# Whole loads of a batch's first x tile, four taps in superblock 4, and transposes moved apart in superblocks 8 to 11

## The chip, the cores and the metric

The kernel runs on one core of a Trainium2 chip. The core has TensorE (matmuls; its weight loads are listed as PEld), VectorE (DVE), ScalarE (ACT), GpSimd (POOL) and SyncE (SP, which here only issues DMAs), and 16 DMA engines that all queues share. The metric is the device time of one execution in microseconds. Of the kernel before, 8 executions were timed: median 751.04 us, from 749.45 to 758.43.

## The reference

Two steps on 32768 tokens (8 batches of 4096) of 192 features. The first is a causal convolution with 7 taps, whose weights differ for each token and each of 8 heads and are a softmax over the taps. The second is a feed-forward layer of width 2048 with `h - tanh(h)` between its two matrix products.

```python
# x: (8, 4096, 192); weight_gen: (8, 4096, 8 heads, 7 taps); group = 24 features of a head
w = softmax(weight_gen, axis=-1)
x_pad = concatenate([zeros((B, 6, D)), x], axis=1)     # a batch begins with six zero rows
x_unf = x_pad[:, arange(S)[:, None] + arange(7)[None, :], :]
y = einsum('bshk,bskhg->bshg', w, x_unf.reshape(B, S, K, H, group))
h = y.reshape(32768, 192) @ w_in                       # 192 x 2048
out = (h - tanh(h)) @ w_out                            # 2048 x 192
```

## The kernel before

**Tiling.** The tokens are cut into 32 superblocks of 1024, four to a batch, numbered n = 0 to 31. Partition p of a tile holds 8 consecutive tokens. A superblock's x tile has 6 more rows in front (the halo), so partition p also has the six tokens before its own; in a batch's first superblock (n = 0, 4, 8, ...) partition 0 has zeros there.

**The convolution of one superblock.** ScalarE takes the exponentials of the weights (line 154), VectorE sums them, takes the reciprocals and scales (lines 168, 183, 214). GpSimd multiplies x by the weights, tap by tap, into bf16 products (line 255): taps 0 to 3 into `pa`, taps 4 to 6 into `pb`. From n = 4 on (`HELP`) VectorE does the eighth token of taps 0 and 1 (line 289). Then the products are added over the taps in two ways together. Some additions are accumulating DMAs issued on GpSimd's queue (`dma_sum`, line 221). The rest is done by TensorE: it transposes each remaining tap's products by multiplying with an identity and accumulates them in PSUM (line 338, 24 matmuls a tap). How many taps are left for TensorE depends on n:

- n in `PART` (2, 3, 4): one sum inside `pa`, taps 0 and 1 plus taps 2 and 3 (768 KB), issued before `pb`'s product. TensorE transposes taps 4, 5, 6, 0, 1.
- n = 5 to 12: one sum of `pb` into `pa[0:3]` (1152 KB), issued after `pb`'s product. TensorE transposes taps 3, 0, 1, 2.
- n in `TWO_SUMS` (13 to 31): that sum and, a superblock later (`second_sum`), `pa[2:4]` into `pa[0:2]`. TensorE transposes two.

The result is evicted from PSUM into `convT` (line 364) in two pieces: `t2`, chunks 0 and 1 of the 192 features, and `t1`, chunk 2.

**The feed-forward layer.** The main loop of superblock n runs over 16 f tiles of 128 hidden features. For each, `gemm1` writes `ph` with 6 matmuls (line 381), ScalarE takes the tanh (394), VectorE subtracts into `gt` (395). The second product runs a superblock behind as a stream of pairs of matmuls into two PSUM banks `obank` (line 417), evicted by ScalarE (436) and stored by SP (440), one store a superblock. `ph` and the transposes' `pc` share three PSUM slots in turn.

**What sets the order.** The schedule is by hand: each engine runs its instructions in program order. A plan says how many output pairs follow each f tile (`pairs`), at which f tile and after how many pairs each transpose piece of superblock n + 1 is put (`t1`, `t2`), and where VectorE's softmax sums and scale stand. `FIRST` is for n = 1, `STEADY` for all others:

```python
STEADY = dict(pairs=(5, 11, 0, 16, 4, 12, 6, 10, 0, 6, 10, 8, 8, 8, 8, 16), t1=(14, 8), t2=(13, 0), scale=14, sums=(1, 13))
```

GpSimd runs ahead: during superblock n it makes the products of n + 2. On SP's queue stand, in program order, the loads of x (n + 3) and of later weights, and the store of n - 1. Up to n = 8 the loads come after the store in the program, from n = 9 on before it. An x load waits for its slot (two x tiles) and, by a manual dependency (`x_after`), for GpSimd's first product of the superblock before.

**A batch's first x tile** is loaded by four DMAs: partitions 16 to 127 whole, partitions 0 to 15 without halo, the halo of partitions 1 to 15, and zeros for the halo of partition 0 (lines 121 and 131, called at 143 to 149).

## Time and profile before

| | |
|---|---|
| median of 8 executions | 751.04 us |
| the profiled execution | 750.1 us |
| its span in the trace | 748.3 us |
| mean granted TensorE clock | 0.998 |
| HBM read, written | 54.49 MB, 25.17 MB |

The span is the time between the first and last instruction recorded; the rest of the execution lies around it. A slice is a fortieth of the span. A digit is the busy share in tenths, where 9 is 90% or more; PEclk is the clock granted to TensorE, in tenths of its full speed.

```profile
PE   3899999999999989999999999999999999999997
...
DVE  7999899989999969999999999999999999988893
ACT  4888888888888868898989989898898989888882
POOL 7999999999999999999999999999999999992000
PEclk9999999999999999999999999999999999999999
DMA  8926636865667669887779878787988877776112
```

The costliest groups have line, engine, operation, written and read tiles, shapes and count; then busy time and mean duration of one; then idle time just before and what ended it:

```profile
L395 DVE TENSOR_TENSOR gt<-ph,th 128x1024 bf16<-128x1024 f32 x512 | 602.3, 1219 | 40.5 <-ACT th L394 27.3
L394 ACT ACTIVATE th<-ph 128x1024 f32<-128x1024 f32 x512 | 514.3, 1026 | 70.3 <-PE ph L381 59.5
L381 PE MATMUL ph<-convT,w_in 64*128 64x512 bf16 x3072 | 419.5, 379 | 4.9 <-DVE gt L395 3.4
...
L417 PE MATMUL obank<-w_out,gt 64*128 64x192 bf16 x7936 | 410.6, 243 | 4.9 <-issue 4.6
L255 POOL TENSOR_TENSOR pa<-x_t,wsm 128x3072 bf16<-128x3072 f32 (+2 forms) x63 | 341.7, 5657 | 0.2
```

Two matmuls run at a time on the two halves of TensorE's rows, so the durations of lines 381 and 417 overlap and their sum is more than TensorE's busy time.

The DMAs by what they move, with the count, the size of one and the median time from issue to landing:

```profile
x_t<-in_x_dram SPq DMA_DIRECT2D x24, 1344.0 KB, 8.1
pa<-pb POOLq DMA_DIRECT2D x27, 1152.0 KB, 9.5
out_dram<-out_sb SPq DMA_DIRECT2D x31, 768.0 KB, 4.3
pa<-pa POOLq DMA_DIRECT2D x22, 768.0 KB, 7.4
x_t<-in_x_dram SPq DMA_DIRECT2D x7, 1176.0 KB, 9.5
```

### The profile page before, as it was taken

The page shows a single profiled execution, that of the slowest core. Times are in us where ns is not written, and L with a number is a line of the kernel's source. Part 1 is how long each engine was busy: PE and PEld are TensorE (multiplying, and loading weights), DVE is VectorE, ACT ScalarE, POOL GpSimd, SP SyncE. Part 2 cuts the span into 40 slices and gives each one's busy share as a digit, 9 for nine tenths or more (in the row PEclk, how much of TensorE's full clock was granted, in tenths as well). Part 3 has the DMA queues.
Part 4 walks back from the last instruction along what each step waited for, and adds up shares of the span by engine and source line. Part 5 has one row for each costly group of instructions (what it writes and reads, how often), then busy time and mean ns, then how long its engine had stood idle before and what let it go on. Part 6 is the DMA issues. An engine that isn't in the chain of part 4 may idle for free.

```text
span 748.3 us, 30081 instructions
## 1 busy us (share of the span) xinstructions
PE 724.0 (97%) x13640; PEld 559.7 (75%) x13640; DVE 684.6 (91%) x711; ACT 640.2 (86%) x872; POOL 657.8 (88%) x158
## 2 busy tenths in 40 slices
PE   3899999999999989999999999999999999999997
PEld 2477777777777777777777777787777777877777
DVE  7999899989999969999999999999999999988893
ACT  4888888888888868898989989898898989888882
POOL 7999999999999999999999999999999999992000
PEclk9999999999999999999999999999999999999999
DMA  8926636865667669887779878787988877776112
GB/s 237 241 46 159 173 116 178 193 170 136 166 167 176 178 173 216 186 217 172 194 207 221 210 199 204 170 201 205 228 193 189 212 179 191 193 148 110 45 44 86
DMA packets 34464, 129.64 MB, mean 173 GB/s; under 512 B 4808, under 2 KB 9656, under 8 KB 30480
## 3 DMA queue, kind: packets, MB, share of 16 engines
q0 software_dynamic: 19296, 50.73, 39.5%
q1 hardware_dynamic: 15040, 77.00, 29.6%
q8 instruction: 106, 1.74, 1.0%
q14 instruction: 22, 0.18, 0.1%
HBM read 54.49 MB, written 25.17 MB: 106 GB/s over the span
## 4 chain that ended last, share of the span: by engine, by line
PE 94%; DVE 3%; issue 1%; ACT 1%; DMA 0%
PE obank L417 44%; PE ph L381 44%; PE pc L338 4%; PE po L460 1%; DVE gt L395 1%; DVE pa L255 1%; ACT th L394 1%; DVE pb L255 0%; DMA wg_t<-in_weight_gen_dram 0%; DVE obank L196 0%; DVE zsum L168 0%; PE obank L338 0%; DVE wsm L214 0%; DVE obank L214 0%; ACT wg_t L154 0%
## 5 line engine op out<-in xcount | busy, mean ns | idle before, releaser
L395 DVE TENSOR_TENSOR gt<-ph,th 128x1024 bf16<-128x1024 f32 x512 | 602.3, 1219 | 40.5 <-ACT th L394 27.3
L394 ACT ACTIVATE th<-ph 128x1024 f32<-128x1024 f32 x512 | 514.3, 1026 | 70.3 <-PE ph L381 59.5
L381 PE MATMUL ph<-convT,w_in 64*128 64x512 bf16 x3072 | 419.5, 379 | 4.9 <-DVE gt L395 3.4
L417 PEld LDWEIGHTS <-gt 64*128 64x128 bf16 x7936 | 357.5, 94 | 87.4 <-issue 13.0
L417 PE MATMUL obank<-w_out,gt 64*128 64x192 bf16 x7936 | 410.6, 243 | 4.9 <-issue 4.6
L255 POOL TENSOR_TENSOR pa<-x_t,wsm 128x3072 bf16<-128x3072 f32 (+2 forms) x63 | 341.7, 5657 | 0.2
L255 POOL TENSOR_TENSOR pb<-x_t,wsm 128x4608 bf16<-128x4608 f32 (+2 forms) x33 | 284.1, 8611 | 0.9 <-ACT wsm L206 0.5
L381 PEld LDWEIGHTS <-w_in 64*128 64x128 bf16 x3072 | 163.6, 94 | 80.3 <-issue 18.4
L436 ACT ACTIVATE out_sb<-obank 128x192 f32<-128x192 f32 x248 | 81.2, 327 | 14.7 <-PE obank L417 14.3
L364 ACT ACTIVATE convT<-pc 128x1024 bf16<-128x1024 f32 (+1 forms) x62 | 50.1, 810 | 1.2 <-PE pc L338 0.7
L221 POOL DMA_DIRECT2D pa<-pb x27 | 34.7, 1284 | 14.5 <-DVE pa L289 7.7
L338 PEld LDWEIGHTS <-pa 64*128 64x128 bf16 x2016 | 41.4, 101 | 6.9 <-DVE pa L255 1.1
L221 POOL DMA_DIRECT2D pa<-pa x22 | 35.8, 1629 | 9.3 <-DMA pa<-pb 8.4
L338 PE MATMUL pc<-ident,pa 64*128 64x64 bf16 x1920 | 40.7, 192 | 1.3 <-DVE pa L255 0.8
L168 DVE TENSOR_REDUCE zsum<-wg_t 128x32 f32<-128x224 f32 (+1 forms) x61 | 23.7, 388 | 2.8 <-ACT wg_t L154 2.8
L154 ACT ACTIVATE wg_t<-wg_t 128x448 f32<-128x448 f32 x32 | 18.3, 571 | 7.1 <-DMA wg_t<-in_weight_gen_dram 7.1
L214 DVE TENSOR_TENSOR wsm<-wg_t,pc 128x448 f32<-128x448 f32 x27 | 16.8, 621 | 3.0 <-DVE pc L183 0.5
L289 DVE TENSOR_TENSOR pa<-x_t,ph 128x384 bf16<-128x384 f32 x28 | 15.5, 554 | 1.2
L183 DVE RECIPROCAL pc<-zsum 128x64 f32<-128x64 f32 x27 | 14.9, 551 | 1.2 <-ACT convT L364 1.2
L338 PE MATMUL pc<-ident,pb 64*128 64x64 bf16 x288 | 6.3, 202 | 8.9 <-POOL pb L255 8.9
L338 PEld LDWEIGHTS <-pb 64*128 64x128 bf16 x360 | 7.8, 105 | 9.6 <-POOL pb L255 8.9
L460 PE MATMUL po<-w_out,gt 64*128 64x192 bf16 x256 | 11.2, 243 | 0.0
(27 smaller groups left out, 55.7 us busy)
## 6 DMA issues: line engine op xcount, KB each, us to landing
x_t<-in_x_dram SPq DMA_DIRECT2D x24, 1344.0 KB, 8.1
pa<-pb POOLq DMA_DIRECT2D x27, 1152.0 KB, 9.5
out_dram<-out_sb SPq DMA_DIRECT2D x31, 768.0 KB, 4.3
pa<-pa POOLq DMA_DIRECT2D x22, 768.0 KB, 7.4
x_t<-in_x_dram SPq DMA_DIRECT2D x7, 1176.0 KB, 9.5
wg_t<-in_weight_gen_dram SPq DMA_DIRECT2D x32, 224.0 KB, 7.2
x_t<-in_x_dram SPq DMA_DIRECT2D x1, 768.0 KB
w_out<-in_moe_w_out_dram POOLq DMA_DIRECT2D x1, 768.0 KB, 9.3
```

Source lines behind the costliest of these rows:

```text
L154: last_exp[0] = nc.scalar.activation(out=wg_t[:].rearrange("p j h k -> p (j h k)"), in_=wg_t[:].rearrange("p j h k -> p (j h k)"), func=AC ...
L168: nc.vector.reduce_sum(out=zsum_of[n][:, j0 * H : j1 * H], in_=e_of[n][:, j0:j1].rearrange("p j h k -> p (j h) k"), axis=AX.X,)
L221: return nc.gpsimd.dma_start(out=out.rearrange("p k j d -> p k (j d)"), in_=in_.rearrange("p k j d -> p k (j d)"), accum_op=mybir.AluOpTyp ...
L255: return eng.tensor_mul(prod(k0, k1)[:, :, j0:j1].rearrange("p k j (h g) -> p k (j h) g", h=H), bass.AP(tensor=x_v.tensor, offset=x_v.offs ...
L338: nc.tensor.matmul(pc[r][:, col : col + R] if home else pc[:, r, col : col + R], lhsT=prods[c][gi][r * R : (r + 1) * R, 2 * j : 2 * j + 2] ...
L364: last_conv[0] = nc.scalar.activation(out=out, in_=pc[:, :, 0:cols].rearrange("p r (cj t) -> p r cj t", t=R), func=ACT.Copy,)
L381: nc.tensor.matmul(ph[:, r, :], lhsT=w_in[r * R : (r + 1) * R, c, f * P : (f + 1) * P], rhs=convT[r * R : (r + 1) * R, c, :], start=(c == ...
L394: last_act[0] = nc.scalar.activation(out=th[:], in_=ph_f, func=ACT.Tanh)
L395: last_sub[0] = nc.vector.tensor_sub(gt[:], ph_f, th[:])
L417: mm = nc.tensor.matmul(po[:, 0:D], lhsT=g_of[n][f][r * R : (r + 1) * R, col : col + P], rhs=w_out[r * R : (r + 1) * R, f, :], start=(r == ...
L436: last_act[0] = nc.scalar.activation(out=out_sb[:, j, :], in_=po[:, 0:D], func=ACT.Copy)
L460: nc.tensor.matmul(po[:, r, 0:D], lhsT=g_of[n][f][r * R : (r + 1) * R, col : col + P], rhs=w_out[r * R : (r + 1) * R, f, :], start=(f == 0 ...
```

## The change

Three edits.

1. *A batch's first x tile* (n = 4, 8, ..., 28) comes in one DMA of 128 partitions with their halo. Partition 0 then holds the last rows of the batch before in its halo. The zeros are written over them by a separate DMA, which the program issues in superblock n - 3 at the first f tile from 8 on after the load. It waits for the load to land.
2. *Superblock 4* leaves `PART`: it has the sum of three taps like superblocks 5 to 12, and TensorE transposes taps 3, 0, 1, 2. It alone is in `LAST_TAP`: GpSimd makes tap 2 before and tap 3 after the sum is issued, instead of both before.
3. *Superblocks 8 to 11* follow a plan `APART`: the pieces `t2` and `t1` of superblocks 9 to 12 stand at f = 10 and f = 15 instead of 13 and 14, the output pairs are spread otherwise (128 in all, as before), and the softmax sums and the scale stand at other f tiles.

```diff
-    PART = (2, 3, 4)
+    PART = (2, 3)
+    LAST_TAP = (4,)
+    X_LATE = ()
+    ZERO_AT = 8
+    RELIEF = ()
...
         else:
-            dma = rows(16 if s == 0 else 0, P)
+            dma = rows(16 if s == 0 and ZERO_AT is None else 0, P)
             if behind is not None:
                 order(dma, behind, "order of the loads")
-            if s == 0:
+            if s == 0 and ZERO_AT is None:
                 rows(0, 16, HALO)
                 rows(1, 16, 0, HALO)
                 no_halo()
+            elif s == 0:
+                halo_of[n] = no_halo
...
-        x_after[n + 1] = mul(nc.gpsimd, 0, KH, 0, J - 1 if n in HELP else J)
-        mul(nc.gpsimd, KH, KA)
-        second_sum(n - 1)
+        first = mul(nc.gpsimd, 0, KH, 0, J - 1 if n in HELP else J)
+        if n in LAST_TAP:
+            x_after[n + 1] = mul(nc.gpsimd, KH, KA - 1)
+            second_sum(n - 1)
+        else:
+            mul(nc.gpsimd, KH, KA)
+            second_sum(n - 1)
+        if n not in LAST_TAP or n not in X_LATE:
+            x_after[n + 1] = first
...
                 dma_sum(pa[:, 0:3], pb[:, 0:3])
+                if n in LAST_TAP:
+                    mul(nc.gpsimd, KA - 1, KA)
...
+    APART = dict(pairs=(4, 12, 0, 16, 0, 16, 4, 12, 0, 16, 4, 12, 0, 6, 10, 16), t1=(15, 5), t2=(10, 2), scale=15, sums=(7, 10))
+    APART_IN = (8, 9, 10, 11)
...
-        plan = FIRST if n == 1 else STEADY
+        plan = FIRST if n == 1 else APART if n in APART_IN else STEADY
...
+            if n + 3 in halo_of and f >= ZERO_AT:
+                halo_of.pop(n + 3)()
             out_pairs(plan["pairs"][f] - done)
```

The diff also adds a function `gemm1_relieved` for f tiles in `RELIEF`; that tuple is empty, so nothing calls it. `X_LATE` is empty as well, so `x_after` keeps its meaning.

In each engine's order of instructions this comes to: TensorE has 24 transposes with their weight loads fewer. GpSimd has one product more, and in superblock 4 its sum stands after `pb`'s product. SP has 14 loads fewer. The zeros of superblock 4 stand directly behind its load; those of 8 behind the load and a load of weights; those of 12, 16, ..., 28 also behind the store that follows. VectorE and ScalarE have the same instructions in another order within superblocks 8 to 11.

## The prediction

> **What bounds the kernel now.** I read the busy shares, the chain that ended last, the chain in order of time, the waits, then single stretches by timeline and by windows. First the page:

> ```profile
> PE 724.0 (97%) x13640; PEld 559.7 (75%) x13640; DVE 684.6 (91%) x711; ACT 640.2 (86%) x872; POOL 657.8 (88%) x158
> ...
> q8 instruction: 106, 1.74, 1.0%
> ...
> PE 94%; DVE 3%; issue 1%; ACT 1%; DMA 0%
> ```

> TensorE is the bound: 94% of the chain. An edit gains only if it removes TensorE work or a stop of TensorE. The chain in order of time shows such stops. One place of each superblock (the two adjacent first-product tiles, f = 8 and 9) comes again and again:

> ```profile
> 140.83 1.43 PE ph L381 x12
> ...
> 165.04 1.43 PE ph L381 x12
> ...
> 187.53 1.38 PE ph L381 x12
> ...
> 232.42 1.38 PE ph L381 x12
> ...
> 254.86 1.38 PE ph L381 x12
> ...
> 282.06 1.34 PE ph L381 x12
> ```

> Superblocks 2 to 4 take about 23 us; then the steps are 24.21 (n = 5 to 6), 22.49, 22.44 on average to 254.86, and 27.20 (n = 10 to 11). From 12 on, where two taps instead of four are transposed, they are about 21.86. So two places lose time: 24.21 - 22.44 = 1.77 us and 27.20 - 22.44 = 4.76 us. The timeline shows the second:

> ```profile
> 264.32 0.34 SPq L121 DMA_DIRECT2D x_t<-in_x_dram  x1
> ...
> 269.36 0.57 PE L417 MATMUL obank<-w_out,gt 64*128 64x192 bf16 x9 [2.87 <-issue]
> 269.37 0.34 PEld L417 LDWEIGHTS <-gt 64*128 64x128 bf16 x8 [3.08 <-issue]
> ...
> 269.97 0.33 ACT L436 ACTIVATE out_sb<-obank 128x192 f32<-128x192 f32 x1 [3.38 <-PE obank L417]
> ```

> TensorE stops inside a run of 32 equal matmuls, released by nothing but "issue", and ScalarE waits for it. The other stop (150.1 to 151.8, 1.69 us) looks the same. Windows of 1 us add what happens meanwhile; after each span stand sum, PE, PEld, DVE, ACT, POOL, granted clock, DMA share, GB/s:

> ```profile
> 267.00:268.00 1.00, 0.00 (x0) 0.00 (x0) 1.00 (x2) 0.00 (x0) 1.00 (x1) 1.00 0.92 369
> 268.00:269.00 1.00, 0.00 (x0) 0.00 (x0) 0.75 (x1) 0.00 (x0) 1.00 (x1) 1.00 1.05 409
> ...
> 271.00:272.00 1.00, 1.00 (x11) 0.68 (x7) 0.33 (x1) 0.64 (x1) 1.00 (x1) 0.50 0.15 43
> 272.00:273.00 1.00, 1.00 (x13) 0.84 (x11) 0.90 (x1) 0.35 (x1) 1.00 (x1) 0.50 0.01 5
> ```

> The DMA engines are full, and after the stop the clock is 0.50 for 3.4 us: 3.08 us of stop and some 1.7 us of slow clock make the 4.76.

> What stops is the supply of instructions. TensorE has 13640 + 13640 instructions; 106 packets of 1.74 MB are 16 KB, 256 instructions, each. The two stops lie 4608 = 18 x 256 instructions apart, on block boundaries. In the trace's packet records block packet j + 1 is sent when TensorE enters block j, and TensorE goes on 1.5 us after it landed. Stop = lag of the packet + its length + 1.5 - time that TensorE needs for a block. At 261.86 TensorE entered a block of 4.43 us; the packet started at 266.91 (lag 5.06) and took 0.95: 5.06 + 0.95 + 1.5 - 4.43 = 3.08, as seen. At 145.39: 3.68 + 1.23 + 1.52 - 4.73 = 1.70.

> The lag is DMA work ahead of it. The tap sum issued by GpSimd at 258.03 moved from 259.9 to 266.9, and the packet began there. The first stop's packet waited in the load of x(8), moving from 143.0. Over the trace, an entry 1.4 us or more after a sum began, and not in its last 2 us, waits 2 to 5 us, to the sum's end or 2 us before; the four entries 0.8 to 1.3 us after its beginning (137.52, 305.25, 480.60, 656.55) did not wait.

> [...]

> **The change part by part.** All is summed against the profiled execution: span 748.3, 1.8 around it, 750.1 in all, 0.94 under the median 751.04.

> *Superblock 4 with four taps.* Transposes go from 120 to 96 matmuls. In the chain "PE pc L338 x80" took 1.17 and "x64" 0.93; with the third chunk's half as many that is 0.24 + 0.12 = **-0.36**. GpSimd: one 3072 product (5.6, from 16.79 for three) becomes two of 2.9: +0.2. The sum moves behind pb's product: products start at 73.62, + 5.3 + 2.9 + 8.4 = 90.2, issue 90.5, and 9.5 to landing (median of its kind) = 100.0. The transposes start at 101.67 and begin with tap 3, which GpSimd ends at 94.2. Cover 1.7 us; each us beyond is a stop of TensorE. pb is then freed by the sum, not by TensorE, which saves the 0.38 that GpSimd waited at 105.30, so superblock 5 is not later.

> *One x load.* Two of four DMAs go, seven times: SP row 140.67 shows 2.29 us for three issues against 0.33. The bytes are the same 1344 KB. The zero write now waits on SP for the load to land. Behind it on SP stand the store of superblock 0 (64.80 before; now behind a load that moves from 59.7 to about 66, so some 3 us later, its buffer needed at 85) and later loads 10 us away. From n = 13 the zeros stand behind the store (issued 319.35): issue 320.4, landing about 324, while GpSimd's product starts at 324.94. No cover to speak of, but if GpSimd is 1 us late, its sums, landing about 12 us before their transposes (357.27 + 7.4 against 377), absorb it. GpSimd's queue keeps its order. Cost 0; bounds 0 and +2 (half a us at each of four batches).

> *Pieces apart.* Same 256 + 96 + 96 matmuls in superblocks 8 to 11. Four pairs of adjacent first-product tiles instead of two: 1.29 to 1.43 for two against 2 x 0.65, so up to 0.13 x 2 x 4 = +1.0. The sums that the earlier transposes at f = 10 need have landed long before (sum of 9 issued at 196.74, + 9.5 = 206; needed about 213). Softmax sums (0.38) and the scale (0.62) only change places; VectorE is busy 21.0 of 22.44 there. The gain is bounded by the same size, as a tile may wait for its PSUM slot at either place. I take 0; bounds -1.0, +1.0.

> *Blocks shift.* 48 instructions fewer put every later boundary 48 instructions later, 24 x 41 ns = 1.0 us among output matmuls (32 take 1.32), less among transposes. Counting instructions with those durations:
> - n = 5: the block entry moves to about 146.5, the next falls due at 150.3. The load is issued faster, so the packet starts between 147 and 149: + 1.05 + 1.5 gives a stop of 0 to 1.3, I take 0.75. **-1.0** against 1.77.
> - n = 10: entry at 17.3 us after the superblock's first matmul (243.2), 260.5, that is 0.6 us after the sum began: served at once. The block, with one transpose piece instead of both, lasts 6.2. **-4.76**.
> - New stops: TensorE is then 4 to 5 us ahead of GpSimd, which alone needs about 21.7 per superblock and catches up only slowly. Sums then lie on the blocks of 5.2 to 6.2 us in superblocks 15 to 21. With the packet at the sum's end each loses 0.3 to 1.0, 4.9 in all; about half of the packets start up to 2 us earlier. I take 3.4, less the 1.6 that superblocks 12 to 30 lose now over 21.86: **+1.8**; bounds 0 and +8.

> Sum: -0.36 - 1.0 - 4.76 + 0 + 0 + 1.8 = -4.3: 745.8 in this execution, **746.7** as a median.

> **The rivals.**
> 1. *Cleaner than that*: no new stops, packets early. For: half of the packets in sums start early. -0.36 - 1.77 - 4.76 = -6.9: 743.2 in this execution, 744.1 as a median; with the gain bound of the pieces 743.1. Chance 0.15.
> 2. *The starvation only moves.* For: at n = 9 an entry falls at 241.5, 2 us into a sum, and at n = 10 0.8 us of lateness puts 260.5 over the 1.4 us limit. Each: 5.06 + 2.45 - 6.15 = 1.4 more, with 1.7 of slow clock if it is longer. Against: the entry at 241.71 had a lag of only 3.54. -4.3 + 2.8 to 4.5: 749.5 to 751.2. A chunk's PSUM slot that waits for one subtract (1.22) in each of four superblocks would give the same. Chance 0.20.
> 3. *Slower: drift onto the sums.* TensorE's lead shifts superblocks 17 to 21 so that entries fall 1.4 to 2.5 us after a sum's beginning, where the lag was up to 5.06. A 5.3 us block then stops 2.2 us, + 1.7 of slow clock = 3.9. Three such (11.7) against -6.1: +5.6, 756.6; it decides from two and a half hits on. Against: each stop sets TensorE back and ends the lead. Chance 0.10.

> My forecast itself (744 to 748.5, from 0 to 1.8 us either way in the last two terms) has 0.55. 0.5% is 3.75 us, about what a measurement of this kernel can tell from no change: below 747.3 is faster. That takes rival 1 (0.15) and, of my own case, the three quarters of 744 to 748.5 that lie below 747.3 (0.40), 0.55 together; same: the rest of it (0.15) and rival 2 (0.20), 0.35; slower: rival 3, 0.10. The range 742 to 752 takes in rivals 1 and 2 and leaves out rival 3.

> **What would show it.** After: 27232 instead of 27280 TensorE instructions, no clock of 0.50 near 270, equal steps from n = 8 to 11, GpSimd's sum of superblock 4 issued near 90.5, stops named "issue" of under 1 us in superblocks 15 to 21. Wrong: a stop over 2 us named "issue" anywhere from n = 5 on; transposes waiting at 101; GpSimd waiting for the zeros by more than 1 us.

## The result, and the profile after

| | median (us) | lowest to highest | executions |
|---|---|---|---|
| before | 750.78 | 749.08 to 758.43 | 32 |
| after | 746.49 | 745.93 to 747.23 | 11 |

The ratio is 0.9933, with a 95% interval of 0.9913 to 0.9952: 4.3 us faster, against 746.7 predicted. The profiled execution of the changed kernel took 747.0 us, with a span of 745.2, 3.1 less than the span before. The spread of the executions also shrank, from 9.3 us to 1.3.

The page of the changed kernel, first busy shares, then the instruction queue, then the chain that ended last:

```profile
PE 722.7 (97%) x13616; PEld 556.9 (75%) x13616; DVE 684.3 (92%) x711; ACT 639.8 (86%) x872; POOL 658.1 (88%) x159
...
q8 instruction: 106, 1.74, 0.9%
...
PE 91%; DVE 4%; DMA 2%; issue 1%; ACT 1%; SPq 0%; DVEq 0%; ACTq 0%
```

TensorE has 24 matmuls fewer and is still the bound; its busy time fell by 1.3 us, and the other 1.8 of the 3.1 us are idle time. The chain in order of time, at pairs of adjacent first-product tiles as before (start, duration, engine, tile written, line):

```profile
231.29 1.29 PE ph L400 x12
...
254.52 1.30 PE ph L400 x12
...
276.98 1.29 PE ph L400 x12
...
299.72 1.39 PE ph L400 x12
```

The steps are 23.23, 22.46 and 22.74 us, where the kernel before had 22.44 and then 27.20: the large loss is gone, and a small one has come at about 248. The timeline shows it (start, duration, engine, line, operation; in brackets the idle time before and its releaser):

```profile
248.72 0.57 PE L466 MATMUL obank<-w_out,gt 64*128 64x192 bf16 x9 [0.60 <-issue]
```

From 25.8 us to the end of the span the clock stays at 1.00: the stretch of 0.50 after 270 is gone. Windows of 1 us of the changed kernel where the kernel before stood still (after the span: PE, PEld, DVE, ACT, POOL, granted clock, DMA share, GB/s):

```profile
268.00:269.00 1.00, 1.00 (x28) 1.00 (x25) 1.00 (x2) 1.00 (x2) 1.00 (x1) 1.00 1.00 406
269.00:270.00 1.00, 1.00 (x14) 0.53 (x11) 1.00 (x2) 1.00 (x4) 1.00 (x2) 1.00 1.04 430
```

The DMA engines are as full as before, but TensorE works through it: its next block of instructions had come already, by a packet that landed at 263.22.

The smaller stop, in superblock 5, is gone as well. Its line in the timeline of the kernel before, and a window of the changed kernel at the same place:

```profile
151.80 0.32 PE L417 MATMUL obank<-w_out,gt 64*128 64x192 bf16 x3 [1.47 <-issue]
```

```profile
150.00:151.00 1.00, 1.00 (x48) 0.90 (x44) 0.28 (x2) 1.00 (x3) 1.00 (x1) 1.00 0.02 5
```

The time by superblocks is taken from the first tanh of one to that of the next, in two profiles of each kernel. The second profiles are the runs e11 and e12 below, taken in one batch.

| superblocks | before | before again | after | after again |
|---|---|---|---|---|
| 0 to 2 | 66.82 | 66.99 | 66.81 | 66.79 |
| 3 and 4 | 46.19 | 47.28 | 46.09 | 45.99 |
| 5 to 7 | 69.15 | 69.40 | 67.89 | 67.94 |
| 8 to 11 | 94.49 | 94.44 | 90.97 | 91.33 |
| 12 to 30 | 416.87 | 417.67 | 418.83 | 417.67 |

The gain lies in 5 (24.20 to 22.50) and in 8 to 11. The first pair of profiles gives back 1.96 us in 12 to 30, above all in superblocks 16 to 19 and 24. The second pair gives back nothing there, but only in the balance: the changed kernel has stops in 16 to 19 again, and the kernel before now loses as much elsewhere.

### The profile page after: what moved, and what is told of

The parts are those of the page before. It is cut to its first block, busy times and chain, and to the rows that moved or that the text cites. A ratio compares the mean times of both kernels' runs of the same rounds, so it can differ in the third digit from the quotient of the medians.

```text
span 745.2 us, 30014 instructions
## 1 busy us (share of the span) xinstructions
PE 722.7 (97%) x13616; PEld 556.9 (75%) x13616; DVE 684.3 (92%) x711; ACT 639.8 (86%) x872; POOL 658.1 (88%) x159
## 3 DMA queue, kind: packets, MB, share of 16 engines
q8 instruction: 106, 1.74, 0.9%
## 4 chain that ended last, share of the span: by engine, by line
PE 91%; DVE 4%; DMA 2%; issue 1%; ACT 1%; SPq 0%; DVEq 0%; ACTq 0%
PE obank L466 43%; PE ph L400 43%; PE pc L357 4%; DVE gt L414 3%; DMA wg_t<-in_weight_gen_dram 2%; PE po L509 1%; DVE pa L265 1%; ACT th L413 1%; DVE zsum L178 0%; SPq L129 0%; DVE obank L206 0%; ACT convT L375 0%; DVE pb L265 0%; SPq L139 0%; ACT out_sb L485 0%
## 5 line engine op out<-in xcount | busy, mean ns | idle before, releaser
L265 POOL TENSOR_TENSOR pa<-x_t,wsm 128x2688 bf16<-128x2688 f32 (+2 forms) x64 | 341.9, 5580 | 0.2
L357 PEld LDWEIGHTS <-pb 64*128 64x128 bf16 x288 | 6.3, 106 | 9.6 <-POOL pb L265 9.1
```

The source lines that it names most:

```text
L265: return eng.tensor_mul(prod(k0, k1)[:, :, j0:j1].rearrange("p k j (h g) -> p k (j h) g", h=H), bass.AP(tensor=x_v.tensor, offset=x_v.offs ...
L357: nc.tensor.matmul(pc[r][:, col : col + R] if home else pc[:, r, col : col + R], lhsT=prods[c][gi][r * R : (r + 1) * R, 2 * j : 2 * j + 2] ...
```

## The experiments

### Each edit alone

**e1, the one x load alone.** On the changed kernel:

```diff
-    PART = (2, 3)
-    LAST_TAP = (4,)
-    APART_IN = (8, 9, 10, 11)
+    PART = (2, 3, 4)
+    LAST_TAP = ()
+    APART_IN = ()
```

> The kernel before with edit 1 alone (a batch's first x tile in one DMA, zeros over its halo). Supply theory (TensorE stops where a block of 256 instructions arrives late behind DMA bursts; edits act by moving block boundaries and bursts against each other): no boundary moves; the load of x(8) ends about 0.7 to 1.3 us sooner, so the stop near 150 shrinks from 1.7 us to 0 to 0.8, the stop near 266 stays at 2.9 to 3.1 us with a clock of 0.50 behind it; 749.3 to 750.5 us against 750.8. Rival (each edit saves by its own work, here fewer DMAs): most of the 4.3 us of the whole change is here, 746.5 to 748.

Measured: 747.59 (746.97 to 747.95, 9 executions), ratio 0.9936 [0.9909, 0.9964]. That is a gain of 3.8 us, more than the theory expected; the time lies in the range of the rival. The profile speaks against the rival all the same: the stop at 150 shrinks to 0.26 us and superblock 5 takes 22.77 instead of 24.20, while superblocks 12 to 30, in which four more such loads run, take 417.06 against 416.87. Near 265 and 287 TensorE still stands for 2.14 and 1.87 us. What the prediction lacked stands in the table of queues on the page, where the columns are packets, MB, and share of 16 engines' span. Before:

```profile
q1 hardware_dynamic: 15040, 77.00, 29.6%
```

With the one load alone:

```profile
q1 hardware_dynamic: 14718, 77.03, 27.8%
```

The bytes are the same, the time is not: 0.296 x 748.3 - 0.278 x 745.7 = 14.2 us less on the engines, 2.0 for each of the seven loads. For x(8) with its weights the packets' own times say the same: they moved for 7.24 us before, 4.75 here.

**e2, superblock 4 alone**, and **e3, the pieces apart alone:**

```diff
-    ZERO_AT = 8
-    APART_IN = (8, 9, 10, 11)
+    ZERO_AT = None
+    APART_IN = ()
```

> The kernel before with edit 2 alone (four taps in superblock 4): 24 transposes fewer, all later block boundaries 48 instructions later. Supply theory: 0.1 to 0.4 us from the transposes, the stop near 150 goes or shrinks (-1.0 to -1.7), and in superblock 10 the boundary comes to about 18.1 us after the superblock's first matmul, some 1.5 us into the sum of superblock 12, with a block of 5.6 us: a stop of 0 to 2.3 us instead of 3.1. 746.5 to 749. Rival (own work): only the 0.1 to 0.4 us of transposes, 750.4 to 750.7.

```diff
-    PART = (2, 3)
-    LAST_TAP = (4,)
-    ZERO_AT = 8
+    PART = (2, 3, 4)
+    LAST_TAP = ()
+    ZERO_AT = None
```

> The kernel before with edit 3 alone (transpose pieces at f = 10 and 15 in superblocks 8 to 11). Supply theory: boundaries before superblock 8 stay, so the stop near 150 stays at about 1.7 us; in superblock 10 the block that was late now holds one transpose piece and lasts about 6 us, so the stop near 266 goes; TensorE's lead then brings stops of 0.3 to 1.0 us in superblocks 15 to 21. Superblocks 8 and 9 keep 22.4 to 22.5 us. 747 to 749. Rival (the pieces apart relieve PSUM slots or VectorE): superblocks 8 to 11 each get 0.3 us or more shorter than 22.44, and the stop near 266 need not change.

Measured: e2 749.09 (748.23 to 749.53, 10), ratio 0.9957 [0.9932, 0.9981]; e3 749.55 (747.55 to 752.31, 10), ratio 0.9944 [0.9916, 0.9973]. Both lie a little above what was expected (746.5 to 749, and 747 to 749). In e2 the stop at 150 shrinks to 1.25 us only, and the large one to 1.46, near 268, with a new one of 1.95 near 290: superblock 10 takes 22.44, but 11, which has both, takes 25.92. In e3 the stop near 270 shrinks to 0.55 us, while the one near 152 is 2.44 with a slow clock behind it; superblocks 8 and 9, which have the new plan but no stop, take 22.47 against 22.44. So the load cures the place near 150 and the pieces apart most of the one near 270, at 0.03 a superblock; four taps in superblock 4 alone shrink both and cure neither. The three gains add to 8.0 us and are 4.3 together, so they overlap.

### Each edit taken out of the changed kernel

**e7, without the one load** (`ZERO_AT = None`), and **e8, without the pieces apart** (`APART_IN = ()`):

```diff
-    ZERO_AT = 8
+    ZERO_AT = None
```

> The changed kernel without edit 1 (x tiles of a batch's beginning in four DMAs again). Supply theory: the load of x(8) lasts some 7.4 us instead of 5.5 again, so superblock 5 has a stop of 0.5 to 1.5 us, and those of 9 and 13 become more exposed; the executions spread by several us again; median 747.5 to 750. Rival (edit 1 matters only by its fewer DMAs on SP): within 0.5 us of 746.5.

```diff
-    APART_IN = (8, 9, 10, 11)
+    APART_IN = ()
```

> The changed kernel without edit 3 (the plan of before in superblocks 8 to 11). Supply theory: the boundaries of edit 2 alone, with the shorter loads of edit 1: no stop in superblock 5, a stop of 1 to 3.5 us at the end of superblock 10 or 11 where both pieces lie in one block; 747.5 to 749.5. Rival (the pieces relieve PSUM or VectorE): each of superblocks 8 to 11 longer by 0.3 us or more than in the changed kernel, without a stop.

Measured: e7 747.85 (746.80 to 748.55, 4), ratio 0.9955 [0.9938, 0.9972]; e8 747.55 (747.17 to 749.50, 5), ratio 0.9957 [0.9941, 0.9973]. In e7 superblocks 8 to 11 run without a stop at 22.46 or 22.47 each, and superblock 5 has its stop back. Its timeline, and a window of it:

```profile
152.85 0.44 PE L357 MATMUL pc<-ident,pa 64*128 64x64 bf16 x11 [2.30 <-issue]
```

```profile
153.00:154.00 1.00, 1.00 (x17) 0.46 (x14) 0.04 (x1) 0.60 (x1) 1.00 (x1) 0.50 0.06 16
```

Edit 2, which is in e7, does not cure this place; the load does. In e8 superblock 11 takes 26.17, while 8 to 10, back on the old plan, take 22.44, no longer than with the new one. The old plan's own work is thus not the loss that the new one removes. The changed kernel without edit 2 alone was not run.

### Only the supply disturbed

**e5, 96 matmuls more at the start of the kernel before**, **e6 and e10, 96 and 112 more at the start of the changed one.** They multiply the identity into a scratch slot before the first convolution, while TensorE waits for the first loads:

```diff
+    idle = psum_h.tile([P, 2, HT], FP32, name="pc", tag="ph")
+    for i in range(96):
+        r = i % 2
+        nc.tensor.matmul(idle[:, r, 0:R], lhsT=ident[r * R : (r + 1) * R, :], rhs=ident[r * R : (r + 1) * R, r * R : (r + 1) * R], start=True, stop=True)
```

> The kernel before with 96 matmuls more on TensorE at its very beginning, before the first transposes, where TensorE waits some 9 us for GpSimd's first product. They write a PSUM slot that nothing reads. With their weight loads they are 192 instructions: every later block boundary falls 192 instructions earlier in the work, and nothing else changes. Supply theory: the time changes by several us, since other blocks meet the DMA bursts; counted with the bursts of the trace of before, blocks in superblocks 3, 9, 10 and 11 are then late by 2 to 4.6 us each: 754 to 763 us. Rival (the stops belong to certain transposes, tiles or the PSUM slots): the same as before within 1 us, stops at the same places.

> The changed kernel with the same 96 matmuls at its beginning. Supply theory: boundaries move as in the run above, but loads are shorter and the pieces are apart in superblocks 8 to 11, so less is lost: stops in superblocks 3 and 9 to 11, 748 to 753 us. Rival: 746.5 within 1 us.

> The changed kernel with 112 matmuls more on TensorE at its beginning: every boundary 224 instructions earlier, so all other blocks meet the bursts. Supply theory: stops at other superblocks than in the changed kernel, in all 2 to 6 us of them as there: 745 to 749. Rival: 746.5 within 0.5 us with the stops at the same superblocks (16 to 19, 24).

Measured: e5 758.4 (755.88 to 762.32, 4), ratio 1.0086 [1.006, 1.0111]; e6 746.3 (746.12 to 746.82, 4), ratio 0.9937 [0.9922, 0.9952]; e10 746.84 (745.46 to 747.41, 6), ratio 0.993 [0.9907, 0.9953].

e5 decides between theory and rival. Superblocks 0 to 2 take 66.97, as before (66.82), so the 96 matmuls cost nothing where they stand; 7.6 us are lost later, with the same work. Expected were 754 to 763, with late blocks in superblocks 3, 9, 10 and 11: these take 25.68, 26.07, 26.18 and 24.34, and 24 and 25 lose time besides. TensorE now stands near 105, 244, 267, 296, 410 and 587. The last of these in the timeline, and windows:

```profile
589.73 0.33 PEld L381 LDWEIGHTS <-w_in 64*128 64x128 bf16 x5 [2.92 <-issue]
```

```profile
588.00:589.00 1.00, 0.00 (x0) 0.00 (x0) 0.75 (x1) 0.00 (x0) 1.00 (x1) 1.00 1.14 225
...
591.00:592.00 1.00, 1.00 (x9) 0.45 (x7) 0.36 (x1) 0.61 (x1) 1.00 (x1) 0.50 0.88 173
```

Here the transfer ahead is a load of x with its weights (581.64 to 589.67), not a sum: the block was entered at about 581.6, and the packet started at 586.56. In the changed kernel the stops move as well (e6: 1.65 us near 106; e10: 2.60 near 105 and 1.27 near 289; neither has one near 248), but the times stay. The 748 to 753 expected of e6 was a miss: two shifts did not ruin the changed kernel. The rival's times came out in e6 and e10, but not its places.

The packet records show the mechanism in every profile. I counted, in all 14, the blocks that TensorE entered after 28 us and finished before 735 us, 1428 in all. TensorE never went on into the next block sooner than 1.20 us after that block's packet had landed. Of the 66 crossings at which its weight loads stood for more than 0.45 us, 65 ended 1.26 to 1.69 us after the landing.

**e4, the tap sum of superblock 12 cut to 16 partitions**, in the kernel before:

```diff
-                dma_sum(pa[:, 0:3], pb[:, 0:3])
+                if n in (12,):
+                    dma_sum(pa[0:16, 0:3], pb[0:16, 0:3])
+                else:
+                    dma_sum(pa[:, 0:3], pb[:, 0:3])
```

> The kernel before, but the accumulating DMA of superblock 12 adds only partitions 0 to 15 (144 KB instead of 1152; the taps 4 to 6 of that superblock are left out of the other partitions, so its output differs). TensorE's instructions and all its waits are the same. Supply theory: the block packet that waited behind this sum from 261.9 to 266.9 starts at once, the stop of 3.1 us and the slow clock behind it go: superblocks 10 and 11 take 22.4 to 22.8 us each, 4 to 4.8 us less together; later small stops give 0 to 2 back; 746 to 748.8. Rival (the stop has another cause: transposes, PSUM, the sequencer): the stop stays, 750.3 to 751.

Measured: 751.75 (747.89 to 756.17, 10), ratio 0.999 [0.9955, 1.0025]; 746 to 748.8 was expected, a miss. The profiled execution had stops ahead of the edited place (superblocks 5, 8 and 9 took 26.90, 25.19 and 24.41), so TensorE came there some 9 us later than in the kernel before and met the sum in another block, the one ahead of the block whose packet had waited. The sum moved from 263.24 to 266.52 only. TensorE entered that block about 1.5 us after it began, and the packet started at 266.32, near the sum's end as before, but now only some 1.6 us after the entry. TensorE works on:

```profile
266.00:267.00 1.00, 1.00 (x22) 0.80 (x20) 1.00 (x2) 1.00 (x2) 1.00 (x1) 1.00 0.08 16
```

Superblocks 10 and 11 take 45.28 instead of 49.61. But the block that had stopped was entered at 271.0, when even a sum of full length (7.0 us in the kernel before) would have been over, and its packet waited 2.5 us in a load of x, for a stop of 0.39. So e4 fits the theory and doesn't show it: neither the place nor the total was a clean test.

### The new plan everywhere, and second profiles

**e9, the plan `APART` in superblocks 5 to 30:**

```diff
-    APART_IN = (8, 9, 10, 11)
+    APART_IN = tuple(range(5, 31))
```

> The changed kernel with the plan of edit 3 in superblocks 5 to 30 instead of 8 to 11. Supply theory: no block holds both transpose pieces any more, the shortest blocks from superblock 5 on last 4.9 to 6.0 us instead of 3.8 to 5.3; the stops of superblocks 16 to 19 and 24 (some 3 us together in the changed kernel's trace) shrink to 0 to 1.5; 744 to 746 us. Rival (the pieces relieve PSUM or VectorE): superblocks without a stop get shorter, below 22.44 in 5 to 7 and below 21.86 from 12 on. Against both: the tap sums come too late for transposes three f tiles earlier, and TensorE waits for a DMA: slower than 746.5.

Measured: 748.43 (748.12 to 750.75, 10), ratio 0.9959 [0.9938, 0.9979]: 744 to 746 was expected, a miss. The chain in order of time, over three superblocks with two transposed taps:

```profile
306.23 1.29 PE ph L400 x12
328.33 1.29 PE ph L400 x12
350.43 1.30 PE ph L400 x12
```

Each step is 22.10, and it stays so up to superblock 29, without a stop over 0.6 us. The objection to both came true once: near 144 TensorE waits 0.72 us for a tap sum, and superblock 5 takes 23.43. But the steps without a stop are 21.86 in the changed kernel. The plan costs 0.24 for each superblock from 13 on, some 4 us in all, more than the stops that it removes.

**e11, all three edits undone, and e12, the changed kernel again**, in one batch, for a second profile of each:

> The kernel before once more (the changed file with all three edits undone, the same instructions on every engine): a second execution to be profiled. If the stops depend on how DMA packets happen to fall, they have other lengths and partly other places here, among superblocks 3, 5, 8 to 11, and the time differs by 1 to 8 us; superblocks without a stop take the same time as before within 0.05 us.

> The changed kernel again, on the same chip as the runs above, to compare with: 746 to 747.5 us.

Measured: e11 one execution of 752.75; e12 746.37 (745.85 to 746.96, 5), ratio 0.993 [0.9907, 0.9954]. A sixth execution of e12 took 4276.77 us; it is left out, and its cause is not known. The places repeat, the sizes don't: the kernel before stops for 1.94 and 3.02 us near 152 and 268 (1.69 and 3.08 in the first profile), and also near 85, 106, 495 and 643. The changed kernel again has one near 248 (1.41) and small ones at 419.7 and 441.2.

No version tried is clearly faster than the changed kernel: e6 (746.3), e12 (746.37) and e10 (746.84) lie within each other's spread.

## Why the prediction was right, and where its terms were not

| term | predicted | first pair of profiles | second pair |
|---|---|---|---|
| transposes of superblock 4 (superblocks 3 and 4) | -0.36 | -0.10 | -1.29 |
| stop of n = 5 (superblock 5) | -1.0 | -1.70 | -1.95 |
| (superblock 6, no term) | 0 | +0.44 | +0.49 |
| stop of n = 10 (superblocks 8 to 11) | -4.76 | -3.52 | -3.11 |
| new stops (superblocks 12 to 30) | +1.8 | +1.96 | 0.00 |

The total, -4.3, is that of the medians. The mechanism held. That the total fits to 0.1 us is in part luck: the terms' errors partly cancel, and the spans of the two pairs of profiles differ by 3.1 and by 6.8 us.

**What bounds it.** Right. e5 loses 7.6 us by 192 instructions that take no time of their own, with stops in the four superblocks that were named before, and in 14 profiles TensorE never goes on before its packet has landed, nor sooner than 1.20 us after.

**Superblock 4.** The sum was issued at 90.89 (predicted 90.5) and moved from 92.74 to 100.34; the transposes from 101.89 did not wait, with 1.5 us of cover. The saved 0.36 shows in superblock 3 (22.50 in e7 and e8 against 22.85 in e1), but it does not stay. (In the first profile after, ScalarE waits 0.48 us for weights in superblock 3, so that it takes 23.09. The -1.29 of the second pair is mostly the kernel before, whose superblock 3 took 24.28 there.) TensorE comes to the next transposes earlier and meets the sum of superblock 5. In e8, at 123.82 against 124.49 in e1 (0.37 of it from superblocks 0 to 2, which took 66.40), it waits for the sum itself:

```profile
124.83 0.88 PE L357 MATMUL pc<-ident,pa 64*128 64x64 bf16 x48 [0.59 <-DMA pa<-pb]
```

Superblock 4 takes 23.44 in e7, 23.33 in the changed kernel again and 23.78 in e8, against 23.00 in e1. In e7 and the changed kernel again a block boundary lies in these transposes, and the sum acts through the packet: it started at 123.17 and 123.10, with the sum's end (123.18 and 123.11), and the stops of 0.38 and 0.26 make most of the loss. The prediction gave this sum no line: it asked what the moved sum covers, not what the next one covers once TensorE is earlier.

**One x load.** "The bytes are the same 1344 KB" and "Cost 0" was the step that failed in size. The single load took 1.7 to 2.5 us less for them: 5.55 us in the changed kernel and 4.75 in e1 for x(8) with its weights, against 7.24 before. In the changed kernel x(8) with its weights moved from 143.39 to 148.93 (5.55 us) and the packet started at 147.78, at the early end of the predicted 147 to 149. The stop of n = 5 was put at 0.75 and is 0. It was also put under *Blocks shift*; by e1, e2 and e7 it belongs to the load. The zero write waits on SP, as said, and holds up no load:

```profile
140.88 0.33 SPq L129 DMA_DIRECT2D x_t<-in_x_dram  x1
...
148.88 0.70 SPq L139 DMA_DIRECT2D x_t<-zero  x1
```

GpSimd waits for no zeros.

**Pieces apart.** Cost 0 against a measured 0.03 a superblock: right for superblocks with four transposed taps. With two taps it is 0.24 (e9).

**The stop of n = 10.** Predicted: entry at 260.5, 0.6 us after the sum began, "served at once", in a block of 6.2. The packet records of this one block, with the idle time of TensorE's weight loads as the stop, and the block's own length as the time to the next entry less the stop:

| kernel | entry, after the sum began | lag of the packet | block's own length | stop |
|---|---|---|---|---|
| before | 261.86, 1.97 | 5.06 | 4.4 | 3.08 |
| e2 (old plan) | 261.49, 1.52 | 4.67 | 5.5 | 1.46 |
| e8 (old plan) | 260.62, 0.88 | 4.81 | 5.5 | 1.69 |
| e3 (new plan) | 264.63, 2.84 | 4.21 | 6.1 | 0.55 |
| e9 (new plan) | 261.97, 1.78 | 3.62 | 6.15 | 0 |
| after (new plan) | 261.32, 1.22 | 0.95 | 6.15 | 0 |
| after again (new plan) | 261.83, 1.87 | 3.24 | 6.15 | 0 |

The length came out (6.15), the early service did not: in the second profile the packet waited 3.24 us, and 3.24 + 1 + 1.5 = 5.7 is hidden by the block's length alone. The rule read from four entries, that an entry 0.8 to 1.3 us into a sum doesn't wait, fell in e8 (0.88, lag 4.81); in e1 an entry only 0.16 us into the sum waited 4.17. Two of the four entries had not shown it either: their packets, at 479.26 and 655.12, started before the sums did (479.33 and 655.30). What edit 3 does is to lengthen this block, from 4.4 or 5.5 us to 6.1, and so to cap what a late packet can cost.

**The starvation only moves.** This rival came true in part. As it said, at n = 9 an entry fell 2.1 us into the sum (241.77, sum from 239.66): lag 4.59, a stop of 0.8 us, and 1.41 in the second profile with a lag of 5.22. Superblocks 10 and 11 together kept 1.15 us over 2 x 22.44, where I had none; that is the size missing from the -4.76.

**New stops.** +1.8 against +1.96 and 0.00. The place was right: in both profiles the changed kernel has stops of 0.2 to 0.8 us in superblocks 16 to 19; one of 1.01 in 24, in the first, was not expected. The size differs from execution to execution, in both kernels: over 19 x 21.86 the changed one loses 3.5 and 2.3 us in 12 to 30 (3.4 was put), the kernel before 1.5 and 2.3 (1.6 was put).

**Open.** Why a packet in one execution starts at once and in another at the sum's end. Superblock 6 takes 22.88 to 23.00 in the changed kernel and in e6, e8, e10 and e12, and 22.5 in e1, e2, e3 and e7: in the changed kernel VectorE idles 0.48 us before 160.14 and TensorE waits for it. It was not tracked down. And no run tells why executions of the kernel before differ by 9 us; those with edit 1 or 2 alone differ by 1.0 and 1.3, those with edit 3 alone by 4.8.

## What to carry to other kernels

On an engine with thousands of instructions and full DMA queues, look at its "issue" stops: if they lie multiples of one number of instructions apart, as TensorE's did here (4608 = 18 x 256), compare the instruction queue's packets with the transfers around them, before looking for a dependency. Such a stop shrank here with a shorter transfer ahead of the packet (e1: 1.69 to 0.26 us) and with a block entered just before that takes longer (e3: 3.08 to 0.55), and an edit far ahead moved it (e5); so measure the medians of several versions and read the places in more than one profile. And when an edit makes the bound engine earlier, ask of every later transfer that it waits for how much cover is left.

## What was not expected of the hardware

**One DMA of 128 partitions was faster than the same bytes in four pieces.** x and its weights, 1568 KB, moved in 5.55 and 6.00 us in the changed kernel (4.75 in e1, 5.13 in e8) and in 7.24 to 8.28 with the four pieces (before, e2, e3, e7).

**The slow clock went with the idle time in a window, not with a stop's length.** Stops of 2.98 us (e5, near 244) and 2.74 (e4, near 226) had no slow clock behind them, a stop of 2.08 (e5, near 267) had. The stretches at 0.50 last 3.41 us, and by the clock records the stretches at 1.00 that end in a slow clock are whole multiples of that: 245.76 and 474.45 us in the kernel before, 720.21 in the changed one, are 72.0, 139.0 and 211.0 times 3.413. I laid windows of that length end to end from their edges over all 14 profiles, from some 60 us on, 2802 windows, and took the time without a weight load in each:

| granted clock in the next window | windows | without a weight load in one (us) |
|---|---|---|
| 0.50 | 7 | 2.08, 2.40, 2.41, 2.41, 2.50, 2.71, 2.85 |
| 1.00 | 2795 | at most 2.26, 2.18, 2.17, 2.07, 2.03 |

The two overlap only between 2.08 and 2.26. By the time without a matmul, with the first 60 us counted in, it is 1.87 to 2.80 us before a clock of 0.50 (17 windows) and at most 1.96 otherwise (2958). The stop of 2.98 fell on two windows with 2.03 and 1.65, the stop of 2.08 into one. Some 1.9 to 2.3 us of 3.41 were enough here. By this, and as an estimate, whether a stop costs its own length or some 1.7 us more (4.76 less 3.08 in the kernel before) depends on where the window lies. Whether that is part of the spread of the kernel before was not tested.
